# Exponentials three steps behind with sums by ScalarE, weights in fewer loads, and another order of the tail, in a top-k attention and feed-forward kernel

## The chip, the cores and the metric

One core of one Trainium2 chip. The metric is the time of one execution on the device in microseconds (us); less is better. Several runs of a kernel are given by their median with the lowest and the highest. The engines are named as the profile names them: PE is TensorE's matmul, PEld its weight load, DVE VectorE, ACT ScalarE, POOL GpSimd, SP SyncE (here only a queue for DMA).

## The reference

Eight batches of eight heads, 576 rows and 64 columns per head. Attention keeps only the 32 largest scores of each row; the result feeds a two-layer network with a squared relu.

```python
scores = scale * np.matmul(q, k.transpose(0, 1, 3, 2))
kth = np.partition(scores, -32, axis=-1)[..., -32:-31]
scores = np.where(scores >= kth, scores, -1000000000.0)
scores = scores - np.max(scores, axis=-1, keepdims=True)
attn = np.exp(scores)
attn = attn / (np.sum(attn, axis=-1, keepdims=True) + 1e-09)
out = np.matmul(attn, v)
x = out.transpose(0, 2, 1, 3).reshape(B * S, H * D)          # 4608 x 512
h = np.maximum(x @ w_in, 0.0)                                # 4608 x 2048
return h * h @ w_out                                         # 4608 x 512
```

## The kernel before

**Steps.** Heads go in pairs. The work is cut into U = 144 steps; a step holds two tiles of 128 query rows against all 576 keys of their heads (the list `steps`; a head's last 64 rows are joined with another's). One Python loop over `u` from 0 to 143 writes out the order of every engine by hand: each instruction goes through `pin`, which keeps it in program order on its engine. So an engine never overtakes: what stands behind a waiting instruction waits too. Tiles come from pools with a fixed number of buffers; a new tile waits for the last reader of the buffer that it takes.

**What happens to step w**, and in which turn of the loop:

- *Scores*, turn w - 1 (`scores`, L272). PE multiplies into two PSUM tiles `sc_a` and `sc_b` (L285), one for each half of the keys. ACT copies both into `s` (L294).
- *Candidates*, turn w - 1 and w (`pairs_of` L306, `quads_of` L319, `both` L332, `lesser` L340, `copy_far` L327). DVE takes maxima of pairs (L314, L315), then maxima and minima of quads (L323, L324) into `cat`. The minima of the pairs come from GpSimd (L338, L347), which needs a copy of one PSUM operand that ACT makes (`most`, L330). In the first EARLY = 11 steps DVE computes part of the minima itself (L317) and neither the copy nor the wider form on GpSimd is needed.
- *Top 32*, turn w (`topk`, L356). Four rounds of MAX8 on DVE (L374), with MATCH_REPLACE8 between them (L378), two tiles each. The largest and the 32nd value go to ACT, which negates them (`neg`, L394).
- *Dropping*, turn w + 1 (`drop`, L404). GpSimd writes for each score a number that is huge and negative where the score is below the 32nd (L409, tile `gone_a` or `gone_b`), and a DMA that accumulates adds it to `s` (L413). In the first EARLY - 2 steps GpSimd adds it itself (L411).
- *Exponentials*, turn w + 2 (`exps`, L415). ACT computes exp(s - max) into `w_two` (L417), one instruction for each of the two tiles; a DMA on SP transposes the result into `wT` (`turn`, L424).
- *Products*, turn w + 4 (`products` L796, `weigh` L452). PE multiplies `wT` with the values (L461) into the one PSUM tile `av_ps`. The values carry a 65th column of ones, so column 64 is the sum of the weights. DVE inverts it (`invert`, L473, reciprocal L475), and ACT scales by it into `x_tok` or `x_rem` (`place`, L483, L494).
- *Feed-forward*, spread over later turns (`x_unit`, `block`, `dense`). When a tile of 128 tokens is full it is transposed (L532) and copied (L538); then come 16 products of 128 x 128 per piece into a PSUM tile `gen` (L583), relu (L590) and square (L598) on ACT, and 16 accumulating products into `dn_ps` (L649), copied out and stored.

The order inside turn u is: drop(u - 1); quads and the first top-k round of u; scores(u + 1) with products(u - 4) between its two halves; invert and place of u - 4; exps(u - 2) and their transpose; DMA fetches of later heads (`fetch`); rounds two and three; the pair maxima of u + 1 and ACT's copy `most`; round four; ACT's `neg`; feed-forward pieces; one load of weights.

**Heads and weights.** `prepare` transposes the q and k of a pair of heads on PE and copies them on ACT, at turns given by `due`. The weights are cast while they are loaded, by DMAs that GpSimd issues (`load_weights`, L742): eight for `w_in`, of 64 rows each, and four for `w_out`. Three go out before the loop, then one per turn.

**The tail.** In the last two steps the masks are applied by DVE (`mask`, L419) to exponentials that ACT computes ahead (`early_exps`, L397), because the way over GpSimd and a DMA would be too long; PE transposes them (`turn_by_tensor`). From L873 on the remaining products, the last two tiles of tokens and their feed-forward pieces (`one`, `two`, `three`, `four`, then `fifth`, `sixth` and two more) are written out one by one. `one.bits(n)` gives the next n of the 16 products into `dn_ps` (L631); `homes` are PSUM homes for the first pieces.

Of the kernel before, what the change touches and what calls it, by code (L numbers as in the profile page):

```python
# [13 lines left out]
f32 = mybir.dt.float32  # L14
# [9 lines left out]
def kernel(  # L24
# [20 lines left out]
    def pin(ins):  # L45
        tc.keep_in_program_order(ins)
        return ins
# [80 lines left out]
    def fetch(n):  # L128
        while n and fetches:
            fetches.pop(0)[1]()  # L130
            n -= 1
# [140 lines left out]
    def scores(u, between=None):  # L272
        ps = [ps_sc.tile([128, 2, 512], f32, name=f"sc_{j}") for j in "ab"]
        js = (1, 0) if u < 2 else (0, 1)

        def half(j):
            for x, (i, c, a) in enumerate(steps[u]):
                qT, kT, bd, va = prep[i]
                k0 = j * HALF + 64 * (1 - x)
                if c < 4:  # L280
                    r = slice(64 * a, 64 * a + 64)
                    lhsT, rhs = qT[r, c * 128:(c + 1) * 128], kT[r, k0:k0 + HALF]
                else:
                    lhsT, rhs = bd[:, :], kT[:, k0:k0 + HALF]
                pin(nc.tensor.matmul(out=ps[j][:, x, 0:HALF], lhsT=lhsT, rhs=rhs, start=True, stop=True))  # L285

        half(js[0])
        if not between:
            half(js[1])
        s = scp.tile([128, 2, S], f32, name="s", bufs=4)  # L290
        st[u] = {"s": s, "ps": ps}
        st[u]["cat"] = scp.tile([128, 2, S], f32, name="cat", bufs=2)
        for j in js:
            pin(nc.scalar.activation(s[:, :, j * HALF:(j + 1) * HALF], ps[j][:, :, 0:HALF], AF.Copy))  # L294
            if u == 0 and j == 1:
# [51 lines left out]
        pin(tt(less, less, d["most"][:, 0:n_h, :, :].bitcast(i32).rearrange("p h x n -> p x h n"), op=ALU.subtract))  # L347

    GROUP = 18
    EARLY = 11  # L350
    held_m = {}
    tests = []

# [35 lines left out]
        return u == U - 1 or (u == U - 2 and x == 1)  # L389

    def negate(u, ends):
        neg = small.tile([128, 2, 2], f32, name="neg", bufs=4)
        got = st[u]["ends"] if ends == 2 else st[u]["ends"][:, :, 0:1]
        pin(nc.scalar.activation(neg[:, :, 0:ends], got, AF.Copy, scale=-1.0))  # L394
        return neg

    def early_exps(u, x):  # L397
        d = st[u]
        if "e" not in d:
            d["e"], d["neg_e"] = {}, negate(u, 1)  # L400
        e = d["e"][x] = scp.tile([128, S], bf16, name="e", bufs=3)
        pin(nc.scalar.activation(e[:, :], d["s"][:, x, :], AF.Exp, bias=d["neg_e"][:, x, 0:1]))
# [11 lines left out]

    def exps(u, x):  # L415
        d = st[u]
        pin(nc.scalar.activation(w_two[u % 3][:, x, 0:S], d["s"][:, x, :], AF.Exp, bias=d["neg"][:, x, 0:1]))  # L417

    def mask(u, x):  # L419
        d = st[u]  # L420
# [1 line left out]
                                           in1=d["e"][x][:, :], op0=ALU.is_ge, op1=ALU.mult))  # L422

    def turn(u):  # L424
        wT = scp.tile([128, 9, 128], bf16, name="wT", bufs=3)
        pin(nc.sync.dma_start_transpose(out=wT[:, :, :], in_=w_two[u % 3][:, :, :].rearrange("p x n -> p (x n)")))
        st[u]["wT"] = wT

# [5 lines left out]

    def turn_by_tensor(u, x):
        if "tp" not in st[u]:
            st[u]["wT"] = scp.tile([128, 9, 128], bf16, name="wT", bufs=3)
# [33 lines left out]
        return last_two[u][:, 0:130].rearrange("p (x d) -> p x d", x=2)  # L471

    def invert(u):  # L473
        r = small.tile([128, 2, 1], f32, name="rsum", bufs=4)
        pin(nc.vector.reciprocal(r[:, :, :], sums(u)[:, :, 64:65]))  # L475
        st[u]["r"] = r
# [3 lines left out]

    full = []

    def place(u, by_vec=False):  # L483
        for x, (i, c, a) in enumerate(steps[u]):
            b, pr = pairs[i]
            o, r = sums(u)[:, x, :], st[u]["r"]
            if c < 4:
                if (b, c) not in x_tok:
                    x_tok[b, c] = ffp.tile([128, 512], bf16, name="x_tok", bufs=8)
                h = 4 * (pr // 2) + 2 * a + pr % 2  # L490
                if by_vec:
# [206 lines left out]
    def most_ups(u):  # L698
        if u < U - 26:
            return 1 if downs else 2  # L700
        return 2 if u >= U - 20 or len(ups) > 4 else 1

    def in_gap(u):
        products(u - 4)
        if moves:
            moves.pop(0)()()

# [24 lines left out]

    w_loads = []
    for kh in range(KH):
        for e in range(2):
            rows = moe_w_in.rearrange("(t e a d) n -> t a e d n", t=2, e=2, a=2)[kh // 2, kh % 2, e]
            w_loads.append((w_in[64 * e:64 * e + 64, kh, :], rows))
    for g in range(4):
        rows = moe_w_out.rearrange("(f p) n -> p f n", p=128)[:, 4 * g:4 * g + 4, :]
        w_loads.append((w_out[:, 4 * g:4 * g + 4, :], rows))  # L740
# [14 lines left out]
    def due(i):  # L755
        if i >= NP - 8:
            return 101 + 4 * (i - (NP - 8))
        return first[4 * (i // 4) + 3] - 1 - 4 * (3 - i % 4) if i >= 4 else 3 * i + 2

    def prepare(u):  # L760
        nonlocal coming
# [11 lines left out]
    ones = const.tile([128, 1], f32, name="ones")  # L773
    pin(nc.gpsimd.memset(ones[:, :], 1.0))
    worst = const.tile([128, 1], f32, name="worst")
    load_weights(2)
    scores(0)
    both(0)
    copy_far(0)
# [8 lines left out]
    def ok(w):  # L788
        return 0 <= w < U
# [6 lines left out]
    def products(w):  # L796
        if ok(w):
            for x in range(2):
                weigh(w, x)

    def turn_x(u):
        for b, c in full:
            x_unit(u, b, c)
        full.clear()

    for u in range(U):
# [13 lines left out]
            both(u + 1)  # L820
        if u == 0:
            in_gap(u)
        if ok(u - 4):
            invert(u - 4)
# [3 lines left out]
        if ok(u - 4):  # L828
            place(u - 4)
        turn_x(u)  # L830
        moves.extend(soon_moves)
        soon_moves.clear()
        if ok(u - 2):
            exps(u - 2, 0)
            exps(u - 2, 1)
            turn(u - 2)
        fetch(4 if u < 12 else 3)
        topk(u, (1, 2))
        if u == U - 2:
            while behind:  # L840
# [12 lines left out]
        if u == U - 2:  # L853
            place(u - 3)
            turn_x(u)
            take("d", True)
            early_exps(u, 1)
            moves.pop(0)()()
        topk(u, (3,))
        if casts_next:  # L860
            prepare(u)
# [4 lines left out]
        if u < U - 2:  # L866
            dense(u, 0)
        st[u]["neg"] = negate(u, 2)
        if u < U - 2:
            dense(u, 1)  # L870
        load_weights(1)

    assert len(ups) == 4 and not downs and len(behind) == 1 and not fresh and not moves and not soon_moves  # L873
    by_hand.append(True)
    two_banks = ps_sc.tile([128, 2, 512], f32, name="sc_a")
    homes.extend(two_banks[:, z, :] for z in range(2))
    one, two = ups.pop(0)(), ups.pop(0)()
    behind.pop(0)()
    one.relu()
    three = ups.pop(0)()  # L880
    products(U - 4)
    four = ups.pop(0)()
    for x in range(2):
        exps(U - 3, x)
    turn(U - 3)
    exps(U - 2, 0)
    one.square(nc.gpsimd)
    two.relu()
    two.square(nc.gpsimd)
    early_exps(U - 1, 0)  # L890
    early_exps(U - 1, 1)
    topk(U - 1, (1, 2, 3))
    one.bits(4)
    three.relu()
    three.square(nc.gpsimd)
    while tests:
        pin(tests.pop(0)())
    mask(U - 2, 1)
    mask(U - 1, 0)
    mask(U - 1, 1)  # L900
# [7 lines left out]
    turned(U - 1, 0, False)  # L908
    products(U - 3)
    turn_by_tensor(U - 1, 1)  # L910
    turned(U - 1, 1, True)
    products(U - 2)
    invert(U - 4)
    invert(U - 3)
    invert(U - 2)
    place(U - 2, True)
    products(U - 1)
    invert(U - 1)
    place(U - 4)
    place(U - 3)  # L920
    place(U - 1, True)
    one.bits(2)
    by_hand.clear()
    late.append(True)
    turn_x(U)
    by_hand.append(True)
    move = moves.pop(0)()
    four.relu()
    late.clear()
    four.square()  # L930
    late.append(True)
    one.bits(2)
    move()
    tail.append(0)
# [4 lines left out]
    fifth.square()  # L939
    sixth = ups.pop(0)()  # L940
    sixth()
    one.bits(4)
    ups.pop(0)()()
    one.bits(4)
    ups.pop(0)()()
# [137 lines left out]
```

## Time and profile before

| | |
|---|---|
| median of 3 runs | 905.44 us (904.69 to 906.34) |
| the profiled execution's own time | 910.4 us |
| its span, first to last instruction | 908.3 us |
| mean granted clock of PE | 0.939 |
| accumulating DMA of `gone_b` into `s`, from issue to landing | 4.5 us median |

The page gives, for one profiled execution, the busy time of each engine, the span in 40 slices, the DMA queues, the chain of work that ended last, and the costliest groups of instructions with the idle time of the engine before them. A group's mean duration is the time from an instruction's start to its end; instructions of one engine overlap, so what an instruction takes of the engine's stream is read from the starts of its neighbours, in the chain or in the timeline. Times in the timeline are us from the start of the span.

### The profile page before, as it was taken

To read this page: it belongs to the slowest core of one execution; us is meant where nothing else is said; L and a number is where in the kernel's file an instruction comes from. 1 tells how busy PE (TensorE), PEld (TensorE's weight loads), DVE (VectorE), ACT (ScalarE), POOL (GpSimd) and SP (SyncE) were. 2 spreads that over 40 slices of the span, in tenths; PEclk is the share of its full clock that TensorE was granted. 3 is DMA by queue.
4 is the path that set the end of the run, shared out by engine and by line. 5 is a ranking of instruction groups with operands and counts; after the bars stand their busy time and mean duration, and the time that the engine had idled before them with its cause. 6 is when DMAs were issued, how large, how long until landed. Compare 5 with 4: busy or idle time off the path is not lost.

```text
span 908.3 us, 20985 instructions
## 1 busy us (share of the span) xinstructions
PE 683.6 (75%) x6264; PEld 426.1 (47%) x6264; DVE 878.8 (97%) x3629; ACT 761.2 (84%) x1755; POOL 780.7 (86%) x821
## 2 busy tenths in 40 slices
PE   6675867777777768777777677787777768887886
PEld 3332445444444445454454444554544444554554
DVE  6998999999999999999999999999999999999994
ACT  3564799889988898888998899888998888997894
POOL 7997889988898888888889888888898898899881
PEclk9999899999999998999998999989999899999998
DMA  7699898889988999899999988989799999787771
GB/s 146 105 165 147 189 187 196 191 193 209 196 189 172 193 206 195 186 184 200 198 190 196 197 195 195 193 194 202 183 202 199 198 205 211 151 169 164 166 162 40
DMA packets 290776, 164.78 MB, mean 181 GB/s; under 512 B 258144, under 2 KB 268640, under 8 KB 290656
## 3 DMA queue, kind: packets, MB, share of 16 engines
q1 hardware_dynamic: 267408, 80.29, 46.2%
q0 software_dynamic: 21904, 82.65, 40.7%
q8 instruction: 52, 0.85, 0.4%
q14 instruction: 68, 0.56, 0.2%
q10 hardware_dynamic: 1344, 0.43, 0.2%
HBM read 37.75 MB, written 9.44 MB: 52 GB/s over the span
## 4 chain that ended last, share of the span: by engine, by line
DVE 62%; issue 12%; ACT 7%; PE 4%; POOL 3%; DMA 2%; POOLq 0%; ACTq 0%
DVE m L374 25%; DVE cat L378 17%; DVE sc_b L314 6%; DVE most L315 4%; DVE cat L323 4%; DVE cat L324 4%; ACT s L294 1%; PE sc_b L285 1%; POOL cat L347 1%; DVE rsum L475 1%; ACT rl L590 1%; ACT x_tok L494 1%; DMA s<-gone_a 1%; ACT w_two_a L417 1%; PE gen L583 1%
## 5 line engine op out<-in xcount | busy, mean ns | idle before, releaser
L374 DVE MAX8 m<-cat 128x8 f32<-128x104 f32 (+3 forms) x1152 | 436.7, 419 | 0.0
L378 DVE MATCH_REPLACE8 cat<-m,cat 128x104 f32<-128x104 f32 (+2 forms) x864 | 261.5, 308 | 0.0
L338 POOL TENSOR_TENSOR cat<-s 128x576 int32<-128x576 int32 (+1 forms) x144 | 238.6, 1657 | 2.8 <-ACT s L294 2.8
L347 POOL TENSOR_TENSOR cat<-cat,most 128x576 int32<-128x576 int32 (+1 forms) x144 | 196.0, 1361 | 31.8 <-ACT most L330 10.7
L285 PE MATMUL sc_b<-qkT 64*128 64x288 f32 x512 | 109.9, 505 | 88.2 <-DVE cat L324 84.1
L285 PE MATMUL sc_a<-qkT 64*128 64x288 f32 x512 | 98.2, 457 | 89.4 <-DVE most L315 35.2
L583 PEld LDWEIGHTS <-w_in 128*128 128x128 bf16 x2304 | 144.8, 101 | 41.7 <-issue 19.0
L649 PE MATMUL dn_ps<-w_out,h 128*128 128x512 bf16 x544 | 155.9, 417 | 1.8 <-ACT wide L657 1.8
L583 PE MATMUL gen<-xT,w_in 128*128 128x128 bf16 x1984 | 135.6, 224 | 3.3 <-ACT xT L538 1.8
L409 POOL TENSOR_SCALAR gone_a<-s,neg 128x576 uint8<-128x576 f32 x143 | 107.1, 749 | 15.5 <-ACT neg L394 4.1
L409 POOL TENSOR_SCALAR gone_b<-s,neg 128x576 uint8<-128x576 f32 x142 | 106.3, 749 | 12.2 <-ACT neg L394 0.3
L294 ACT ACTIVATE s<-sc_b 128x576 f32<-128x576 f32 x144 | 93.4, 648 | 27.8 <-PE sc_b L285 24.0
L285 PEld LDWEIGHTS sc_a<-qkT 64*128 64x128 f32 x512 | 41.6, 188 | 116.8 <-issue 35.4
L294 ACT ACTIVATE s<-sc_a 128x576 f32<-128x576 f32 x144 | 91.3, 634 | 3.2 <-DVE cat L317 1.7
L285 PEld LDWEIGHTS sc_b<-qkT 64*128 64x128 f32 x512 | 45.0, 203 | 103.7 <-PE av_ps L461 62.5
L394 ACT ACTIVATE neg<-m 128x4 f32<-128x4 f32 (+1 forms) x145 | 29.9, 206 | 72.0 <-DVE m L374 70.6
L598 ACT ACTIVATE h<-rl 128x512 bf16<-128x512 f32 x137 | 86.3, 630 | 4.3
L590 ACT ACTIVATE rl<-gen 128x512 f32<-128x512 f32 x140 | 81.9, 585 | 1.8 <-PE gen L583 1.7
L461 PEld LDWEIGHTS <-wT 128*128 128x128 bf16 (+1 forms) x1600 | 55.3, 101 | 57.9 <-issue 45.8
L649 PEld LDWEIGHTS <-h 128*128 128x128 bf16 x544 | 52.5, 106 | 63.5 <-issue 29.9
L413 POOL DMA_DIRECT2D s<-gone_b x67 | 59.3, 885 | 22.0 <-DVE m L374 9.9
L413 POOL DMA_DIRECT2D s<-gone_a x66 | 58.3, 884 | 20.4 <-DVE m L374 10.8
(177 smaller groups left out, 1261.0 us busy)
## 6 DMA issues: line engine op xcount, KB each, us to landing
s<-gone_b POOLq DMA_DIRECT2D x67, 576.0 KB, 4.5
s<-gone_a POOLq DMA_DIRECT2D x66, 576.0 KB, 4.6
v_raw<-in_v_dram SPq DMA_DIRECT2D x64, 128.0 KB, 3.1
k_raw<-in_k_dram SPq DMA_DIRECT2D x63, 128.0 KB, 3.3
q_raw<-in_q_dram SPq DMA_DIRECT2D x63, 128.0 KB, 3.0
out_dram<-wide SPq DMA_DIRECT2D x31, 256.0 KB, 3.0
v_raw<-in_v_dram SPq DMA_DIRECT2D x64, 32.0 KB, 3.0
w_in<-in_moe_w_in_dram POOLq DMA_DIRECT2D x8, 256.0 KB, 4.5
```

The source lines that it names most:

```text
L285: pin(nc.tensor.matmul(out=ps[j][:, x, 0:HALF], lhsT=lhsT, rhs=rhs, start=True, stop=True))
L294: pin(nc.scalar.activation(s[:, :, j * HALF:(j + 1) * HALF], ps[j][:, :, 0:HALF], AF.Copy))
L338: pin(tt(less, s[:, :, 0:wide].bitcast(i32), s[:, :, HALF:HALF + wide].bitcast(i32), op=ALU.add))
L347: pin(tt(less, less, d["most"][:, 0:n_h, :, :].bitcast(i32).rearrange("p h x n -> p x h n"), op=ALU.subtract))
L374: pin(nc.vector.max(out=m[r][:, x, :], in_=part(r, x)))
L378: pin(nc.vector.match_replace(out=part(r, x), in_to_replace=m[r][:, x, :], in_values=part(r, x), imm_value=NEG))
L409: pin(nc.gpsimd.tensor_scalar(byte[:, x, :, 1], s[:, x, :], scalar1=d["neg"][:, x, 1:2], scalar2=-HUGE, op0=ALU.add, op1=ALU.mult))
L413: pin(nc.gpsimd.dma_start(out=s[:, :, :].rearrange("p x n -> p (x n)"), in_=byte[:, :, :, :].rearrange("p x n two -> p (x n two)").bitcast ...
L583: pin(nc.tensor.matmul(out=hp[:, n * n_rows:(n + 1) * n_rows], lhsT=w_in[:, kh, (f0 + n) * 128:(f0 + n + 1) * 128], rhs=xt(kh), start=(kh ...
L590: pin(nc.scalar.activation(kept["rl"][:, :], hp, AF.Relu))
L598: pin(nc.scalar.activation(h2, flat, AF.Square))
L649: pin(nc.tensor.matmul(out=op[:, :], lhsT=held["h2"][:, f, c * 128:(c + 1) * 128], rhs=w_out[:, f, :], start=(f == 0), stop=(f == NF - 1)))
```

## The change

- *Exponentials*: `to_raise(u)` gives u - 3 up to turn CATCH = 133 and u - 2 after it; products, invert and place follow one turn later as well (`to_weigh`: u - 5, later u - 4). At turn 133 a second pair of exps is issued, at turn 134 a second set of products. `s` gets five buffers, `wT` four, `neg` six.
- *Sums*: for steps below SUMMED = 120 each exps instruction also writes the sum of its row (`accum_out`) into a small tile that two steps share, and `invert` takes one reciprocal of four numbers per row for two steps. From step 120 on it is as before.
- *EARLY* is 9.
- *Weights*: `w_in` goes in four loads of 128 rows, two of them before the loop; eight loads in all.
- *Fetches* stand ahead of the exps in turns 0 to 5; pairs 2 and 3 are prepared earlier (`due`).
- *Tail*: the first two pieces get a PSUM tile each; a third piece is multiplied earlier; eight `dn_ps` products go out before the transposes of the last exponentials, and four fewer near the end; DVE and ACT share copies and scalings differently; the fourth square goes from ACT to GpSimd.

```diff
-        s = scp.tile([128, 2, S], f32, name="s", bufs=4)
+        s = scp.tile([128, 2, S], f32, name="s", bufs=5)
...
-    EARLY = 11
+    EARLY = 9
...
+    SUMMED = U - 24
...
     def exps(u, x):
         d = st[u]
-        pin(nc.scalar.activation(w_two[u % 3][:, x, 0:S], d["s"][:, x, :], AF.Exp, bias=d["neg"][:, x, 0:1]))
+        if u % 2 == 0 and x == 0 and u < SUMMED:
+            d["sums"] = small.tile([128, 2, 2], f32, name="sums", bufs=4)
+            st[u + 1]["sums"] = d["sums"]
+        total = d["sums"][:, u % 2, x:x + 1] if u < SUMMED else None
+        pin(nc.scalar.activation(w_two[u % 3][:, x, 0:S], d["s"][:, x, :], AF.Exp, bias=d["neg"][:, x, 0:1], accum_out=total))
...
     def invert(u):
+        if u < SUMMED:
+            if u % 2 == 0:
+                both_r = small.tile([128, 2, 2, 1], f32, name="rboth", bufs=4)
+                pin(nc.vector.reciprocal(both_r[:, :, :, 0], st[u]["sums"][:, :, :]))
+                st[u]["r"], st[u + 1]["r"] = both_r[:, 0], both_r[:, 1]
+            return
...
+    CATCH = U - 11
+
+    def to_raise(u):
+        return u - 3 if u <= CATCH else u - 2
+
+    def to_weigh(u):
+        return u - 5 if u <= CATCH + 1 else u - 4
+
     def in_gap(u):
-        products(u - 4)
+        products(to_weigh(u))
...
     for kh in range(KH):
-        for e in range(2):
-            rows = moe_w_in.rearrange("(t e a d) n -> t a e d n", t=2, e=2, a=2)[kh // 2, kh % 2, e]
-            w_loads.append((w_in[64 * e:64 * e + 64, kh, :], rows))
+        rows = moe_w_in.rearrange("(t e a d) n -> t a e d n", t=2, e=2, a=2)[kh // 2, kh % 2]
+        w_loads.append((w_in[:, kh, :], rows))
...
-        return first[4 * (i // 4) + 3] - 1 - 4 * (3 - i % 4) if i >= 4 else 3 * i + 2
+        return first[4 * (i // 4) + 3] - 1 - 4 * (3 - i % 4) if i >= 4 else 2 * i + 3
...
-    load_weights(2)
+    load_weights(1)
...
-        if ok(u - 2):
-            exps(u - 2, 0)
-            exps(u - 2, 1)
-            turn(u - 2)
-        fetch(4 if u < 12 else 3)
+        if u < 6:
+            fetch(4)
+        w = to_raise(u)
+        if ok(w):
+            exps(w, 0)
+            exps(w, 1)
+            turn(w)
+        if u >= 6:
+            fetch(4 if u < 12 else 3)
...
-            early_exps(u, 1)
             moves.pop(0)()()
+        if u == CATCH:
+            exps(u - 2, 0)
+            exps(u - 2, 1)
+            turn(u - 2)
...
+        if u == CATCH + 1:
+            products(u - 4)
+            invert(u - 4)
+            place(u - 4)
+            turn_x(u)
...
-    two_banks = ps_sc.tile([128, 2, 512], f32, name="sc_a")
-    homes.extend(two_banks[:, z, :] for z in range(2))
-    one, two = ups.pop(0)(), ups.pop(0)()
+    homes.extend(ps_sc.tile([128, 2, 512], f32, name=name)[:, 0, :] for name in ("sc_a", "sc_b"))
+    one, two, three = (ups.pop(0)() for _ in range(3))
     behind.pop(0)()
     one.relu()
-    three = ups.pop(0)()
...
-    exps(U - 2, 0)
     one.square(nc.gpsimd)
     two.relu()
     two.square(nc.gpsimd)
+    exps(U - 2, 0)
...
-    one.bits(4)
-    three.relu()
-    three.square(nc.gpsimd)
-    while tests:
-        pin(tests.pop(0)())
+    one.bits(8)
...
-    turned(U - 1, 1, True)
+    turned(U - 1, 1, False)
     products(U - 2)
+    products(U - 1)
+    three.relu()
     invert(U - 4)
     invert(U - 3)
-    invert(U - 2)
-    place(U - 2, True)
-    products(U - 1)
-    invert(U - 1)
     place(U - 4)
     place(U - 3)
-    place(U - 1, True)
-    one.bits(2)
+    three.square(nc.gpsimd)
+    while tests:
+        pin(tests.pop(0)())
+    invert(U - 2)
+    place(U - 2, (True, True))
+    invert(U - 1)
+    place(U - 1, (True, False))
+    four.relu()
+    four.square(nc.gpsimd)
...
     sixth()
-    one.bits(4)
     ups.pop(0)()()
     one.bits(4)
```

More of the change, by code (lines that the diff above doesn't have):

```diff
@@ L391, in negate @@
     def negate(u, ends):
-        neg = small.tile([128, 2, 2], f32, name="neg", bufs=4)
+        neg = small.tile([128, 2, 2], f32, name="neg", bufs=6)
         got = st[u]["ends"] if ends == 2 else st[u]["ends"][:, :, 0:1]
@@ L424, in turn @@
     def turn(u):
-        wT = scp.tile([128, 9, 128], bf16, name="wT", bufs=3)
+        wT = scp.tile([128, 9, 128], bf16, name="wT", bufs=4)
         pin(nc.sync.dma_start_transpose(out=wT[:, :, :], in_=w_two[u % 3][:, :, :].rearrange("p x n -> p (x n)")))
@@ L436, in turn_by_tensor @@
         if "tp" not in st[u]:
-            st[u]["wT"] = scp.tile([128, 9, 128], bf16, name="wT", bufs=3)
+            st[u]["wT"] = scp.tile([128, 9, 128], bf16, name="wT", bufs=4)
             st[u]["tp"] = {}
@@ L481, with place @@
     full = []
-    def place(u, by_vec=False):
+    def place(u, by_vec=(False, False)):
         for x, (i, c, a) in enumerate(steps[u]):
@@ L490, in place @@
                 h = 4 * (pr // 2) + 2 * a + pr % 2
-                if by_vec:
+                if by_vec[x]:
                     pin(nc.vector.tensor_scalar(x_tok[b, c][:, h * 64:(h + 1) * 64], o[:, 0:64], scalar1=r[:, x, :], scalar2=None, op0=ALU.mult))
@@ L822 @@
             in_gap(u)
-        if ok(u - 4):
-            invert(u - 4)
+        if ok(to_weigh(u)):
+            invert(to_weigh(u))
         casts_next = bool(soon) and soon[0].__name__ == "values"
@@ L827 @@
             prepare(u)
-        if ok(u - 4):
-            place(u - 4)
+        if ok(to_weigh(u)):
+            place(to_weigh(u))
         turn_x(u)
@@ L868 @@
         st[u]["neg"] = negate(u, 2)
+        if u == CATCH + 1:
[3 more added lines that the diff above has]
+            turn_x(u)
         if u < U - 2:
             dense(u, 1)
+        else:
+            early_exps(u, 1)
         load_weights(1)
@@ L926 @@
     by_hand.append(True)
+    one.bits(2)
     move = moves.pop(0)()
[L928 to L931, printed above, removed]
     one.bits(2)
```

## The prediction

> **What bounds the kernel now.** I read the page from the top (busy shares, chain, groups), then the windows, then single steps in the chain and the timeline.
>
> ```profile
> span 908.3 us, 20985 instructions
> PE 683.6 (75%) x6264; PEld 426.1 (47%) x6264; DVE 878.8 (97%) x3629; ACT 761.2 (84%) x1755; POOL 780.7 (86%) x821
> DVE 62%; issue 12%; ACT 7%; PE 4%; POOL 3%; DMA 2%; POOLq 0%; ACTq 0%
> ```
> ```profile
> 300.00:400.00 100.00, 75.17 (x696) 47.92 (x694) 99.25 (x409) 87.89 (x202) 87.80 (x88) 0.91 0.89 191
> ```
>
> VectorE (DVE) is 97% busy and 99.25 of 100 us in the middle: it is the bound. ScalarE (ACT, fourth pair of numbers) has 12.1 us per 100 left. A step, from one `L323` to the next, is 6.00 us; one step in the chain:
>
> ```profile
> 302.67 0.36 DVE cat L323
> 303.03 0.36 DVE cat L324
> 303.39 0.33 DVE m L374 x2
> 303.73 0.47 DVE cat L378 x2
> 304.20 0.08 DVE rsum L475
> 304.28 0.36 DVE m L374 x2
> ...
> 308.67 0.35 DVE cat L323
> ```
>
> The reader is to see the difference between a duration and a place in the stream: DVE instructions overlap, and the reciprocal, whose group row gives 156 ns, pushes the next maximum back by 0.08 us only.
>
> **The parts, each against this execution (910.4 us, of which 908.3 are the span).**
>
> *Reciprocals.* 120 steps had one each; now 60 cover two steps each. 60 go: 60 x 0.08 = **-4.8**. Twice the elements (four for two) I cost at nothing. By the 156 ns it would be 9.4; I take the place in the chain and keep 9.4 as an end.
>
> *EARLY from 11 to 9.* The two steps 9 and 10 lose their `L317` on DVE:
>
> ```profile
> 59.82 0.44 DVE L317 TENSOR_TENSOR cat<-sc_a,s 128x288 f32<-128x288 f32 x1
> 60.19 1.40 DVE L374 MAX8 m<-cat 128x8 f32<-128x576 f32 x2
> ```
>
> 0.37 apart, so **-0.7**. ACT gets two `L330`, GpSimd two wider pairs and, for steps 7 and 8, two DMA issues in place of four additions: work that other steps already carry beside a DVE of 6.00 us, cost 0; without that cover 0.4 each.
>
> *Exponentials one step later.* What this removes are waits of ACT for the accumulating DMA:
>
> ```profile
> 78.71 0.95 POOL L413 DMA_DIRECT2D s<-gone_b  x1 [0.31 <-DVE sc_b L314]
> 90.10 1.44 ACT L417 ACTIVATE w_two_a<-s,neg 128x576 bf16<-128x576 f32 x2 [6.52 <-DMA s<-gone_b]
> 91.87 0.46 DVE L323 TENSOR_TENSOR cat<-sc_b,most 128x288 f32<-128x288 f32 x1 [5.55 <-ACT most L330]
> 278.53 0.46 DVE L323 TENSOR_TENSOR cat<-sc_b,most 128x288 f32<-128x288 f32 x1 [0.54 <-ACT most L330]
> ```
> ```profile
> DVE rsum L475 <- PE av_ps L461: 1.1, 2, 0.7
> ```
>
> One DMA took 11.4 us (78.71 to 90.10); ACT had stood ready for its exps since 83.58, 5 us after the issue; in ACT's queue `L330` stood behind them, and DVE waited 5.55. With a step more there are 11 us, so what is left is under 0.4. The second such wait (0.54) goes too. The two waits of the reciprocal for TensorE (1.1 in all) go for another reason: the sum now comes from ACT, steps earlier. What is late next is the transposed tile `wT`; exps to products stays two steps, so that is no worse. Sum **-7.2**, bounds 0 (the DMA is not slow in other executions) and -7.2.
>
> *The cost: 240 exps write a sum.* The built program has one ACT instruction more behind each of them, which reads the accumulator, for steps 0 to 119. The trace has none. The nearest row is the smallest ACT instruction:
>
> ```profile
> 308.71 0.21 ACT L394 ACTIVATE neg<-m 128x4 f32<-128x4 f32 x1 [0.69 <-DVE m L374]
> 308.82 0.58 ACT L590 ACTIVATE rl<-gen 128x512 f32<-128x512 f32 x1
> 305.42 1.45 ACT L417 ACTIVATE w_two_a<-s,neg 128x576 bf16<-128x576 f32 x2
> ```
> ```profile
> L417 ACT ACTIVATE w_two_a<-s,neg 128x576 bf16<-128x576 f32 x96 | 69.6, 786 | 7.2 <-DMA s<-gone_b 7.2
> L394 ACT ACTIVATE neg<-m 128x4 f32<-128x4 f32 (+1 forms) x145 | 29.9, 206 | 72.0 <-DVE m L374 70.6
> ```
>
> It holds the stream for 0.11 us and lasts 0.21. Lower end 0 (hidden in the exp's own end), upper end 0.30 (its whole 0.21, and most of the 0.12 by which two exps of 0.786 overlap in 1.45). I take 0.10 as nearest, 0.20 per step. It is free only where ACT is early. The place that decides is `L330`, which stands right behind the exps and which DVE's `L323` waits for:
>
> ```profile
> 307.08 0.41 ACT L330 ACTIVATE most<-sc_b 128x288 f32<-128x288 f32 x1 [0.21 <-DVE sc_b L314]
> 308.59 0.44 DVE L323 TENSOR_TENSOR cat<-sc_b,most 128x288 f32<-128x288 f32 x1
> ...
> 314.17 0.41 ACT L330 ACTIVATE most<-sc_b 128x288 f32<-128x288 f32 x1
> 314.62 0.46 DVE L323 TENSOR_TENSOR cat<-sc_b,most 128x288 f32<-128x288 f32 x1
> ```
>
> Here 1.10 us of room in one step, 0.04 in the next. Over the 110 steps from 10 to 119 (first and last pair: 78.69 and 80.24, 740.98 and 742.20) the room averages 0.68; it is under 0.2 in 15 steps, under 0.4 in 23, under 0.5 in 33. What is missing sums to 2.2 us for 0.2 more per step, 6.0 for 0.4, 8.8 for 0.5. Lateness that ACT's idle time in a step does not absorb goes into the next; carrying it gives 2.7, 9.7 and 14.8. So **+2.7**, bounds 0 and 21 (0.3 per read).
>
> *Catch-up at step 133, spare buffers, fetches ahead of exps, preparation earlier.* The extra exps (1.45) and products stand on ACT around one `neg`, where ACT waits for DVE 70.6 us in all (row above), and early ACT is busy for 15.98 of 25 us:
>
> ```profile
> 25.00:50.00 25.00, 16.97 (x106) 8.57 (x105) 25.00 (x101) 15.98 (x38) 23.45 (x27) 1.00 0.66 122
> ```
>
> Cost 0; if that cover is gone, 1.5. A transpose on SP now stands behind four fetches in steps 0 to 5, with two steps until its products.
>
> *Weights in four loads.* POOL saves four issues of 0.57; it is not the bound, 0. The bytes are the same. The rival below is about the engines that carry them.
>
> *Tail.* Near the end the chain is TensorE without a gap:
>
> ```profile
> 895.45 0.86 PE dn_ps L631 x4
> 896.31 0.89 PE end L583 x16
> 897.20 0.86 PE dn_ps L631 x4
> 898.07 0.89 PE gen L583 x16
> ```
>
> One of the two `dn_ps` groups moves ahead of the last transposes: -0.86. Before that, ACT waited for both halves of one PSUM tile:
>
> ```profile
> 883.43 0.60 ACT L590 ACTIVATE rl<-sc_a 128x512 f32<-128x512 f32 x1 [1.45 <-PE sc_a L583]
> 887.44 1.54 DVE L421 SCALAR_TENSOR_TENSOR w_two_c<-s,m,e 128x576 bf16<-128x576 f32 x2 [0.74 <-ACT e L402]
> ```
>
> With two tiles the relu starts 16 products (0.89) sooner, and with it the exps and `e` behind it on ACT; DVE has 0.74 of idle for `e` to give, and the chain from the masks to the xT copy moves up by about 0.9. The new wait: eight `dn_ps` products in a row wait for GpSimd's second square, with the transposes of `w_two_b` queued behind on TensorE; that square comes sooner too, as its relu moves ahead of one exp, and I take it that the products end when the masked tile is ready. **-1.8**; bounds 0 (the eight products hold the transposes up by the 0.9) and -2.3.
>
> **Sum.** -4.8 - 0.7 - 7.2 - 1.8 + 2.7 = -11.8: 910.4 becomes 898.6. Against the median of the runs shown, 905.44, the profiled execution is 5.0 longer. If those 5.0 are part of the 7.2 of waits, 2.2 are left to gain in a run without a profile: 905.44 - 4.8 - 0.7 - 2.2 - 1.8 + 2.7 = 898.6. Both ways lead to the same; I say **898.6**.
>
> **The rivals.**
>
> *The waits are in every run* and the 5.0 is the profiler's own: 905.44 - 11.8 = 893.6. For it: the three runs agree within 1.7 us, as they would with a regular stall. Against: one DMA that lasts 11.4 where the median is 4.5 looks like chance.
>
> *ACT becomes the bound (slower).* At `L423`, if a read costs 0.25, 0.5 per step: 14.8 in place of 2.7 gives 910.7; at 0.2, 9.7, 905.6. It decides from about 0.21 on, where the cost eats the other gains. For it: an `L394` lasts 0.21, and the accumulator can be read only after the exp has ended. Against: short ACT instructions overlap, 0.11 apart.
>
> *The large w_in loads run on few DMA engines.* Their source is two blocks of 64 rows, their destination 128 partitions. If such a load is dealt out by its two blocks, two engines carry 64 rows each:
>
> ```profile
> q0 software_dynamic: 152, 0.52, 54.7%
> ```
> ```profile
> q0 software_dynamic: 48, 0.18, 90.5%
> q1 hardware_dynamic: 7, 0.00, 1.1%
> ```
>
> From 8 to 14 us a packet of queue 0 took 0.547 x 16 x 6 / 152 = 0.35 us, so a load would hold its engines for 22 us instead of 3, until about 46 us for the last; and from 11.2 to 12.2 us, with that queue full, the q, k and v loads of queue 1 got 1.1%. The third pair's loads are wanted by its transposes,
>
> ```profile
> 37.70 0.66 PE L174 MATMUL gen<-id_f,q_raw 128*128 128x128 f32 x4
> ```
>
> and these move from step 4 to step 3, to about 31 us, a step earlier. An engine held from 8 to 30 us then still has most of that pair's packets to carry: about 3 us late, and as much for the fourth pair while the last load runs. Not all of it passes on to DVE: +4, bounds 0 and 8, so 902.6. The Trainium skill, "DMA: Bandwidth & Descriptors", section "Why a DMA increments its semaphore by 16 and not by 1", states such a rule: the largest number up to 16 that divides the slowest dimension of both sides, 2 here; it also names software-issued copies that get 16 all the same. The same page's "Rules for kernel authors" would have one transfer over 128 partitions and gives no gain for halves; by that alone the sum stays. No load of before has such a shape, so no row here decides.
>
> **How the numbers follow.** Forecast 0.48; waits in every run 0.14; costly reads 0.17 (slower 0.09, same 0.06, still faster 0.02); few engines 0.15 (faster 0.11, same 0.04); the rest, a tail or a phase that does not gain, 0.06 (faster 0.04, same 0.02). Faster by over 0.2% (about what a measurement of this kernel can tell from no change): 0.79, same 0.12, slower 0.09. The range reaches from the second case with cheap reads, 891, to reads of 0.2, 906.
>
> **What would show it.** DVE steps of 5.92 and 6.00 us in turn until step 119 and 6.00 after; no `L323` waiting over 1 us; an ACT group of 240 accumulator reads, 0.1 apart from what follows; exps without a DMA as releaser; the final run from the xT copy to the end shorter by 0.86. I am wrong if steps grow beyond 6.1 us until step 122 and shrink after it (reads), if packets of w_in still run after 40 us (engines), or if the transposes of `w_two_b` wait for a square (tail).

## The result and the profile after

The changed kernel takes 914.81 us (median of 6 runs, 913.76 to 918.18); the kernel before, on the same chip, 905.29 (904.33 to 907.53). The ratio is 1.0106 (95% interval 1.0086 to 1.0126): slower by 9.5 us, where 6.8 less than the median was forecast. The profiled execution of the changed kernel took 914.7 us, so it stands near its median; that of before stood 5 above.

First the head of the changed kernel's page, with its chain:

```profile
span 912.6 us, 20980 instructions
PE 671.4 (74%) x6190; PEld 424.8 (47%) x6268; DVE 873.8 (96%) x3567; ACT 779.4 (85%) x1996; POOL 778.2 (85%) x816
DVE 66%; issue 12%; ACT 10%; PE 5%; SPq 5%; DMA 2%; ACTq 0%
```

DVE does 5 us less work than before (878.8), as the removed instructions would have it, and yet the span is longer. New in the chain is SyncE's queue (SPq) with 5%, but that part of the chain hangs on a releaser that the landing times below do not bear out, so nothing is built on it here. To place the loss, take `L323` at the start of steps 8, 120 and 142 from the two timelines, before first:

```profile
61.52 0.43 DVE L323 TENSOR_TENSOR cat<-sc_b,most 128x288 f32<-128x288 f32 x1
...
742.20 0.43 DVE L323 TENSOR_TENSOR cat<-sc_b,most 128x288 f32<-128x288 f32 x1
...
874.53 0.45 DVE L323 TENSOR_TENSOR cat<-sc_b,most 128x288 f32<-128x288 f32 x1
```
```profile
77.39 0.44 DVE L323 TENSOR_TENSOR cat<-sc_b,most 128x288 f32<-128x288 f32 x1
...
747.85 0.43 DVE L323 TENSOR_TENSOR cat<-sc_b,most 128x288 f32<-128x288 f32 x1
...
881.30 0.43 DVE L323 TENSOR_TENSOR cat<-sc_b,most 128x288 f32<-128x288 f32 x1
```

Up to step 8: +15.9. Steps 8 to 120: 670.5 in place of 680.7, -10.2. Steps 120 to 142: +1.1. From there to the end of the span: 31.3 in place of 33.8, -2.5. The sum is +4.3, the difference of the spans. So the middle and the tail gained, and all that was lost was lost in the first 77 us. Of the 10.2 some 7 belong to that one execution of before: in e3_before_large, which has the steps of before from 8 to 120, the stretch lasts 673.8. The waits of the changed kernel from 30 to 62 us, each row with its total, count and longest:

```profile
ACT qkT L175 <- PE gen L174: 17.5, 2, 14.1
PE gen L174 <- DMA q_raw<-in_q_dram: 17.0, 2, 13.5
DVE sc_b L314 <- ACT s L294: 15.8, 1, 15.8
POOL gone_b L411 <- ACT neg L394: 15.1, 1, 15.1
PEld gen L174 <- DMA k_raw<-in_k_dram: 13.8, 1, 13.8
PEld gen L174 <- DMA q_raw<-in_q_dram: 3.9, 1, 3.9
```

It is one stall of 15.8 us in step 4: DVE waits for ACT, ACT for TensorE's transposes, and these for the third pair's q (3.5 us) and then for its k (13.5 us):

```profile
35.45 0.63 PE L174 MATMUL gen<-id_f,q_raw 128*128 128x128 f32 x4 [3.47 <-DMA q_raw<-in_q_dram]
49.61 1.11 PE L174 MATMUL gen<-id_f,k_raw 128*128 128x128 f32 x4 [13.54 <-DMA q_raw<-in_q_dram]
```

The PE rows put the second wait down to a q load, the PEld rows to a k load. PEld is right: these transposes read `k_raw`, and the pair's second large k load, issued at 27.41, landed 22.2 us later, at 49.57. Why q and k are late stands in SyncE's timeline, of the changed kernel first, then of before. The columns are start, the time that the issuing instructions took, and how many they are:

```profile
12.03 1.82 SPq L110 DMA_DIRECT2D q_raw<-in_q_dram  x2
13.89 10.85 SPq L117 DMA_DIRECT2D q_raw<-in_q_dram  x1
24.79 6.74 SPq L110 DMA_DIRECT2D k_raw<-in_k_dram  x2
31.57 1.98 SPq L117 DMA_DIRECT2D k_raw<-in_k_dram  x1
33.66 1.23 SPq L108 DMA_DIRECT2D v_raw<-in_v_dram  x2
34.93 6.05 SPq L117 DMA_DIRECT2D v_raw<-in_v_dram  x2
41.08 6.03 SPq L110 DMA_DIRECT2D q_raw<-in_q_dram  x2
49.59 1.23 SPq L117 DMA_DIRECT2D q_raw<-in_q_dram  x1
```
```profile
12.06 1.24 SPq L110 DMA_DIRECT2D q_raw<-in_q_dram  x2
13.35 0.67 SPq L117 DMA_DIRECT2D q_raw<-in_q_dram  x1
14.05 0.60 SPq L110 DMA_DIRECT2D k_raw<-in_k_dram  x1
...
29.81 0.59 SPq L110 DMA_DIRECT2D k_raw<-in_k_dram  x1
30.45 0.64 SPq L117 DMA_DIRECT2D k_raw<-in_k_dram  x1
```

The third pair's q goes out at 12.03 and its k at 24.79 to 31.57; what goes out at 41.08 is the fourth pair's q. The DMA view gives the time from issue to landing of these loads, two rows of the changed kernel first (issues from 8 to 14 and from 26 to 32 us), then the same of before:

```profile
q_raw<-in_q_dram SPq DMA_DIRECT2D x2, 128.0 KB, 22.7
k_raw<-in_k_dram SPq DMA_DIRECT2D x2, 128.0 KB, 20.3
```
```profile
q_raw<-in_q_dram SPq DMA_DIRECT2D x2, 128.0 KB, 5.9
k_raw<-in_k_dram SPq DMA_DIRECT2D x1, 128.0 KB, 4.5
```

So q was issued as early as before and landed 17 us later: the transfer is slow. The issue is slow too: one 32 KB load takes 10.85 us to issue in place of 0.67, and SyncE issues in order. This pushes k's first load from 14.05 to 24.79, but its last ones, at 29.81 and 30.45 in before, by little. How much of k's lateness comes from the late issue and how much from the slow transfer is not separated in this kernel; g1_one_two_block and h1_alone below say more. What fills the DMA engines meanwhile is in the DMA view, changed kernel from 8 to 48 us, and 8 to 14 us in the last two rows (columns: issues and KB each, then median us from issue to landing; for a queue packets, MB and share of 16 engines):

```profile
w_in<-in_moe_w_in_dram POOLq DMA_DIRECT2D x4, 512.0 KB, 24.6
```
```profile
q1 hardware_dynamic: 2685, 0.82, 58.1%
q0 software_dynamic: 923, 0.06, 15.1%
```

A load of twice the bytes takes 24.6 us where 4.5 was the median in the same stretch of before. And queue 0 carries 923 packets with 0.06 MB, where before it carried 152 with 0.52: most of them are packets of 4 bytes. From 8 to 62 us the trace holds 3680 such packets, for 6 weight loads; the run by halves below has 128 for 8 loads, 16 each. 3680 - 6 x 16 = 3584 = 4 x 14 x 64: each two-block load gives 14 engines 64 packets without data, and leaves 64 rows to each of the other two. The trace does not name the engine of a packet, so this is read from counts. A second count agrees: of the 4 KB packets of queue 0, 2.0 are in flight on average from 12 to 14 us, some 6 from 20 to 24, when three loads are under way, 7.9 from 26 to 32, with four, and 2.0 again from 40 to 46, with the last one: two per load.

### The profile page after: what moved, and what is told of

Same layout as the page of the kernel before. It is cut to its first block, busy times and chain, and to the rows that moved or that the text cites. A ratio compares the mean times of both kernels' runs of the same rounds, so it can differ in the third digit from the quotient of the medians.

```text
span 912.6 us, 20980 instructions
## 1 busy us (share of the span) xinstructions
PE 671.4 (74%) x6190; PEld 424.8 (47%) x6268; DVE 873.8 (96%) x3567; ACT 779.4 (85%) x1996; POOL 778.2 (85%) x816
## 4 chain that ended last, share of the span: by engine, by line
DVE 66%; issue 12%; ACT 10%; PE 5%; SPq 5%; DMA 2%; ACTq 0%
DVE m L374 28%; DVE cat L378 18%; DVE sc_b L314 6%; DVE most L315 5%; DVE cat L324 5%; DVE cat L323 5%; SPq L117 2%; ACT s L294 2%; SPq L110 1%; ACT h L610 1%; DMA q_raw<-in_q_dram 1%; ACT rl L602 1%; PE dn_ps L661 1%; PE sc_b L285 1%; PE gen L595 1%
## 5 line engine op out<-in xcount | busy, mean ns | idle before, releaser
L285 PE MATMUL sc_b<-qkT 64*128 64x288 f32 x512 | 105.8, 488 | 87.6 <-DVE cat L324 83.6
L595 PEld LDWEIGHTS <-w_in 128*128 128x128 bf16 x2304 | 149.0, 102 | 41.5 <-issue 20.3
L661 PE MATMUL dn_ps<-w_out,h 128*128 128x512 bf16 x478 | 143.0, 421 | 10.6 <-issue 6.8
L595 PE MATMUL gen<-xT,w_in 128*128 128x128 bf16 x1984 | 137.6, 226 | 3.5 <-ACT xT L550 2.9
L411 POOL TENSOR_SCALAR gone_b<-s,neg 128x576 uint8<-128x576 f32 x142 | 105.9, 746 | 29.1 <-ACT neg L394 17.5
L294 ACT ACTIVATE s<-sc_b 128x576 f32<-128x576 f32 x144 | 93.2, 647 | 22.2 <-PE sc_b L285 16.3
L314 DVE TENSOR_TENSOR sc_b<-sc_a,s 128x288 f32<-128x288 f32 x144 | 65.3, 454 | 18.8 <-ACT s L294 16.3
L661 PEld LDWEIGHTS <-h 128*128 128x128 bf16 x544 | 51.8, 105 | 64.0 <-issue 31.3
## 6 DMA issues: line engine op xcount, KB each, us to landing
w_in<-in_moe_w_in_dram POOLq DMA_DIRECT2D x4, 512.0 KB, 24.6
```

Source lines behind the costliest of these rows:

```text
L314: pin(tt(far, one[:, :, QUAR:HALF], two[:, :, QUAR:HALF], op=ALU.max))
L411: pin(nc.gpsimd.tensor_scalar(byte[:, x, :, 1], s[:, x, :], scalar1=d["neg"][:, x, 1:2], scalar2=-HUGE, op0=ALU.add, op1=ALU.mult))
L595: pin(nc.tensor.matmul(out=hp[:, n * n_rows:(n + 1) * n_rows], lhsT=w_in[:, kh, (f0 + n) * 128:(f0 + n + 1) * 128], rhs=xt(kh), start=(kh ...
L661: pin(nc.tensor.matmul(out=op[:, :], lhsT=held["h2"][:, f, c * 128:(c + 1) * 128], rhs=w_out[:, f, :], start=(f == 0), stop=(f == NF - 1)))
```

## The experiments

Letters in the expectations: A, a two-block load is carried by two DMA engines and blocks the loads behind it; B, the accumulator reads ate the gain; C, large loads as such; D, the earlier preparation. F and G came later. All edits are to the changed kernel if nothing else is said; "before" is its run on the same chip. The groups of runs were measured on different chips, on which the kernel before took 905.18 (e1 to e4), 904.92 (f1 to f4), 904.22 (f5, f6, g1, g2) and 903.83 us (h1, h2), so a difference of about 1 us between runs of different groups shows nothing.

**Eight loads again (e1_eight).** The loop of before in place of the new one, and `load_weights(2)` ahead of `scores(0)`.

> The changed kernel (914.8 us) with w_in in eight loads of 64 rows again. Theory A (a two-block load is carried by two DMA engines and blocks the q, k and v loads): step 4 goes back from 22.2 us to about 6.3, w_in lands in about 4.5 us, and the time is 914.8 - 15.8 = 899.0 (897 to 901). Theory B (the accumulator reads cost what was lost): no more than 2 us are gained, 913. Theory D (the earlier preparation of the third pair is what stalls): step 4 still stalls by several us, 905 to 915.

Measured: 904.03 us (897.45 to 907.96 without the profiled execution, which took 919.5); ratio 0.9963 (0.9928 to 0.9999). Step 4 took 6.30 us and w_in landed in 4.6, as A has it. But the time is 5 above A's and scatters over 10 us. The profiled execution, the longest of all eleven, lost 22 us in steps 10 to 13, in the chain at

```profile
66.12 11.46 DMA wT<-w_two_c
77.58 11.96 DMA wT<-w_two_a
...
94.97 19.66 DMA wT<-w_two_c
```

A second thing is wrong in this kernel; it is taken up by f4_eight_early11. That the shorter executions lose their time at the same place is not shown.

**Four large loads of another shape (e2_by_halves).**

```diff
-    for kh in range(KH):
-        rows = moe_w_in.rearrange("(t e a d) n -> t a e d n", t=2, e=2, a=2)[kh // 2, kh % 2]
-        w_loads.append((w_in[:, kh, :], rows))
+    for t in range(2):
+        for e in range(2):
+            rows = moe_w_in.rearrange("(t e a d) n -> t e d a n", t=2, e=2, a=2)[t, e]
+            w_loads.append((w_in[64 * e:64 * e + 64, 2 * t:2 * t + 2, :], rows))
```

> The changed kernel with four loads of 512 KB still, but each into 64 partitions with two rows of 4 KB per partition, so that the slowest dimension is 64 and not 2. Theory A: no stall in step 4, landing 7 to 10 us (twice the bytes of the 4.5 us loads), 899 (897 to 902). Theory C (large loads as such fill the engines): the landing stays above 20 us and so does the stall, 910 to 915.

Measured: 897.31 us (896.34 to 899.18); before 905.18; ratio 0.9903 (0.9876 to 0.9930). The DMA view from 8 to 48 us and the windows of 30 to 50 us, this run first, then the changed kernel (DVE is the third pair of numbers):

```profile
w_in<-in_moe_w_in_dram POOLq DMA_DIRECT2D x4, 512.0 KB, 6.8
```
```profile
30.00:40.00 10.00, 7.51 (x38) 3.99 (x38) 10.00 (x46) 6.49 (x17) 9.40 (x11) 1.00 0.73 113
40.00:50.00 10.00, 6.32 (x51) 3.42 (x51) 10.00 (x36) 7.00 (x19) 9.31 (x12) 1.00 1.15 174
```
```profile
30.00:40.00 10.00, 1.86 (x8) 1.10 (x8) 10.00 (x45) 2.00 (x4) 7.53 (x9) 0.81 0.89 154
40.00:50.00 10.00, 0.39 (x2) 0.39 (x3) 0.14 (x1) 0.00 (x0) 0.00 (x0) 0.50 0.64 115
```

The same number of loads, the same bytes, packets of 4 KB in both: what differs is which dimension stands outermost, and with it the number of partitions that a load fills (64 in place of 128), and 17.5 us come back. The partitions are not it: the loads of w_out, 512 KB into 128 partitions too, land after 6.6 us in the kernel before. C falls, A stands. This kernel computes all that the reference asks and is faster than both.

**The large loads in the kernel before (e3_before_large).** The two-block loop and one load ahead of `scores(0)`.

> The kernel before (905.3 us) with the four two-block loads alone. Theory A: SyncE's issues block as in the changed kernel, q of the third pair lands at about 49 us where its transposes want it at 37.7, so the time grows by 9 to 16, to 914 to 921. Theory D: the preparation is not earlier here, so no stall: 905. Theory B: 905.

Measured: 924.52 us (923.31 to 926.10), ratio 1.0202 (1.0142 to 1.0262): +19.3, more than A's 16. Step 4 took 25.0 us and step 5 8.2 in place of 6.3 each. What TensorE waited for here was not q, as A has it, but a transposed tile `wT`, for 19.8 us: its issue stood 13.2 us in SyncE's queue, and it landed 26.5 us after the issue began. B and D fall: the loads alone cost it all.

**Preparation where it was (e4_due).** `due` back at `3 * i + 2`, large loads kept.

> The changed kernel with the large loads kept and the preparation of pairs 1 to 3 put back to where it was (one step later for the third pair). Theory A: the landing of q sets the end of the stall, whichever step asks for it, so at most 3 us come back: 911 to 915. Theory D: 899.

Measured: 915.68 us (914.98 to 916.93). The stall only moves to step 5 (24.2 us in place of 6.4). D falls.

**The price of the sums (f1_no_sums, f2_sums_unused),** on the loads by halves.

```diff
-    SUMMED = U - 24
+    SUMMED = 0                      (f1)
-        if u < SUMMED:
+        if u < 0:                   (f2, in invert alone)
```

> The changed kernel with the w_in loads by halves (897.3 us), but without the sums: no exp writes a sum, and each step takes its own reciprocal from PSUM again (120 in place of 60). By the forecast's terms 60 reciprocals at 0.08 come back (+4.8) and 240 reads at 0.10 go (-2.7): 899.4. If the reads are free: 902.1. If a read costs 0.25 (-14.8): 887.

> As the run without sums, but the 240 exps still write their sums, which nobody reads; 120 reciprocals from PSUM. Against the loads by halves (897.3) only the reciprocals differ: +4.8 by their place in the stream, 902.1; +9.4 by their duration, 906.7. Against the run without sums only the accumulator reads differ: +2.7 by the forecast, 0 if they are free, +14.8 if ScalarE is the bound.

Measured: 901.49 (900.14 to 902.47) without sums, 903.11 (900.61 to 906.47) with sums that nobody reads, ratios 0.9957 (0.9941 to 0.9973) and 0.9980 (0.9961 to 0.9998). So 240 reads cost 1.6 (from step 8 to 120, by `L323`: 674.2 and 676.0), and 60 reciprocals 5.8 against the loads by halves (676.0 and 670.5). The intervals of the two ratios overlap a little, and one trace tells little: in the ten other traces of kernels with sums and with exponentials three steps behind (e1_eight with its jam left out) this stretch lasts from 669.1 to 672.0. So the reciprocals' gain is clear, and the price of the reads is small, but not clear of noise. A pair of exps with their reads in ACT's timeline of the changed kernel:

```profile
309.09 0.78 ACT L423 ACTIVATE w_two_b<-s,neg 128x576 bf16<-128x576 f32 x1
309.76 0.21 ACT L423 ACTIVATION_READ_ACCUMULATOR w_two_b<-s,neg 128x1 f32 x1
309.85 0.78 ACT L423 ACTIVATE w_two_b<-s,neg 128x576 bf16<-128x576 f32 x1
310.52 0.20 ACT L423 ACTIVATION_READ_ACCUMULATOR w_two_b<-s,neg 128x1 f32 x1
310.61 0.41 ACT L330 ACTIVATE most<-sc_b 128x288 f32<-128x288 f32 x1
```

A read lasts 0.21 us, but what follows starts 0.09 after it: its place in the stream is 0.09.

**Exps two steps behind (f3_two_behind),** on the loads by halves: `CATCH = -99`.

> The loads by halves (897.3) with the exponentials two steps behind all the way, as in the kernel before, and so no catch-up at step 133. By the forecast's second way (most of the waits for the accumulating DMA occur in the profiled run of before alone) 0 to 2.2 come back: 897.3 to 899.5. If the waits are in every run (the rival): 904.5.

Measured: 900.21 us (898.55 to 901.45), ratio 0.9949 (0.9932 to 0.9966): by the medians the third step is worth 2.9, its catch-up included. Its waits show what it removes, here the largest two of five such groups; in the run by halves one wait of 1.7 is left:

```profile
ACT w_two_b L423 <- DMA s<-gone_a: 4.6, 4, 1.6
ACT w_two_a L423 <- DMA s<-gone_a: 3.6, 5, 1.3
```

Many waits of about 1 us, and none of 5. How they reach DVE the trace does not show: its `L323` waits 1.8 us for `L330` here and 1.6 in the run by halves.

**Eight loads, EARLY 11 (f4_eight_early11).** e1_eight with `EARLY = 11`.

> The changed kernel with eight loads of w_in (median 904.0, runs from 897.4 to 908.0) and EARLY at 11 again, so that the accumulating DMAs begin in step 9 and not in step 7, when the last w_out load is gone. Theory F (the jam of steps 10 to 13 in that run is w_out loads, which eight w_in loads push to step 8, beside the accumulating DMAs that EARLY 9 brings forward): narrow runs near 897.3 + 0.7 = 898.0 (897 to 899.5). If eight loads are at fault by themselves: again 903 to 905, with the same spread.

Measured: 897.81 us (897.21 to 899.15). The scatter is gone. In e1_eight the last two w_out loads went out at 63.05 and 69.63 and the first accumulating DMAs at 65.80 and 72.36; here the DMAs begin at 78.61. So with EARLY 9 the loads must be few: four of them bring the last w_out load forward to 50.63.

**EARLY by itself (f5_halves_early11, g2_halves_early7),** on the loads by halves.

> The loads by halves (897.3 us) with EARLY back at 11. By the forecast two DVE minima of 0.37 come back: 898.0. If EARLY 9 also costs somewhere (two more copies on ScalarE, two more accumulating DMAs): 897 or less.

> The loads by halves (897.3 us) with EARLY at 7, so that the first accumulating DMA goes out at about 52 us, while the last w_out load (50.6 to 57) is under way. Two more minima saved: 896.6 if nothing jams. By theory F (w_out loads beside accumulating DMAs jam): over 899 with a spread of several us, as the eight loads with EARLY 9 had, though with one load beside them in place of two.

Measured: 898.08 (896.34 to 902.19) with 11, 897.31 with 9, 897.46 (896.05 to 898.58) with 7. From 11 to 9 the medians differ by 0.8, within the spread and across two chips; in the traces the two steps are shorter by 0.37 and 0.36, as forecast. From 9 to 7 nothing is gained. F in its simple form falls: with 7 an accumulating DMA went out at 52.87 beside a w_out load from 50.12, and nothing jammed. In e1_eight two of each went out within 10 us; how many it takes stays open.

**The tail's four products (f6_bits),** on the loads by halves: `one.bits(8)` becomes `one.bits(4)`, and `one.bits(4)` stands behind `sixth()` again.

> The loads by halves (897.3 us) with the four dn_ps products of the tail moved back to where they stood before (behind the sixth group instead of ahead of the transposes). By the forecast +0.86: 898.2. If the eight products hold the transposes up by as much: 897.3.

Measured: 898.50 us (896.32 to 901.39). From `L323` of step 142 to the end of the span 31.7 us in place of 31.3: 0.4 by the trace, where the medians say 1.2 and the spread and the change of chip cover both.

**One two-block load (g1_one_two_block).** The first quarter of w_in as in the changed kernel, the second in two loads of 64 rows, the other half by halves.

> The changed kernel with one two-block load (the first) and the other three quarters of w_in in loads of 64 partitions. Theory A (each two-block load holds two engines for some 22 us, and SyncE's issues stand behind them): packets of the one load end at about 33 us instead of 47 for four, q of the third pair lands some 14 us sooner, so step 4 stalls by 0 to 2 us: 897.3 to 899.5. If one such load blocks as long as four: 912.

Measured: 910.65 us (909.19 to 912.48). A miss: one load costs 13.3, four 17.5. TensorE waits 12.7 us for the third pair's q here and only 0.9 for its k. The two large q loads went out at 12.02 and 12.62, as in before, and landed some 30 us later, so SyncE's slow issue, which came behind them, has no part in this wait. The DMA view from 20 to 26 us (the busy share of the 16 engines in tenths, and GB/s):

```profile
DMA  2011110203011130111111112011111199990251
GB/s 61 0 41 27 34 27 7 61 0 68 0 34 27 29 89 2 34 27 29 34 29 34 29 61 56 0 29 27 29 29 29 27 166 84 84 166 0 58 82 29
```

In most slices two engines of 16 (one tenth) move 29 GB/s and little else moves. 512 KB at 29 GB/s is 18 us, but the jam lasts longer: the same rate holds again from 36 to 40 us, after the two-block load has landed at 34.7, as if two engines still had shares of other loads to carry. Two runs asked why.

**That load alone, and that load last (h1_alone, h2_last).** h1 holds all other weights back until step 4 (`if u >= 4: load_weights(1)`, no second load ahead of the loop, `EARLY = 13`); h2 sends the same five loads with the two-block one last.

> One two-block load of w_in as in the run with one, but all other weights are held back until step 4 and later (and EARLY is 13, so that w_out does not meet the accumulating DMAs: about 1.5 us more in steps 9 to 12). Theory G (the shares of the other weight loads stand behind it on its two engines): the pair is free at about 8.5 + 18 = 27 us plus the shares of q, k and v, SyncE's blocked issues end before 32 us, and the stall in step 4 falls from 12.5 to 4 or less. If one load blocks by itself: the stall stays at 10 to 13.

> The same five loads of w_in, the two-block load last, at about 30 us, when the third pair's q, k and v have been issued (they were issued by 28 us in the run with loads by halves). Theory G: no stall in step 4; its pair of engines is held from 30 to about 48 us, so the next pair's loads, w_out and the transposed tiles meet it there, with a stall of 0 to 8 us in steps 5 to 7. If the place makes no difference: 12 us in steps 5 to 7.

Measured: h1 901.34 us (899.36 to 905.43), of which some 1.5 belong to EARLY 13; step 4 takes 7.4 us, a stall of 1.1 in place of 12.5. Of the 4.0 us against the loads by halves, measured on another chip, the rest stays open. The load itself still lands after 24.7 us, and the issue behind it still takes 10.86, as in g1_one_two_block, but TensorE's wait for q falls from 12.7 to 1.6. So G holds: one load jams so long because the shares of the loads behind it queue on its two engines. h2: 914.12 us (913.32 to 914.92, two runs). Step 4 is free, as expected, but steps 5 and 6 stall by 14.7 and 1.8: TensorE waited 16.2 us for a transposed tile `wT`, which landed 23.1 us after its issue. More than the 8 expected; the place changes who waits, and does not make it cheaper.

## Why the prediction was wrong, point by point

- *Weights in four loads*: the step that failed. "POOL saves four issues of 0.57; it is not the bound, 0. The bytes are the same." The number of issues and bytes was counted, not how a load is dealt out to the engines; measured, a loss of 15.8 in the trace (step 4) and of 17.5 against as many loads by halves. The cause in its place: each load lies on two engines for some 24 us, and the loads of q and k behind it land 20 to 23 us after their issue in place of 4 to 6.
- *The rival "few DMA engines"* had the right mechanism and the wrong size and chance: +4 with bounds 0 to 8, at 0.15. It reckoned the load's hold of its engines well (22 us; 24.6 to landing) and its sign came, with packets of w_in until 47 us. It put the third pair about 3 us late, and q was: TensorE waited 3.5 us for it. What it left out is k, 13.5 us more: k's large loads were issued at 24.79 and 27.41, behind the fourth two-block load (23.59, landed at 47.7), and landed at 43.3 and 49.6. Part of this is SyncE's slow issue (10.85 us); in the run by halves the same loads go out at 15.28 and 15.87. But the slow issue is not needed for a stall: g1_one_two_block has one of 12.5 us from q loads issued on time.
- The rule that this rival named, in the Trainium skill, "DMA: Bandwidth & Descriptors", section "Why a DMA increments its semaphore by 16 and not by 1", is borne out by the counts: 2 divides the two blocks and the 128 partitions, and two packets with data are in flight per load. The Trainium skill asks on the same page, under "Rules for kernel authors", in another row for a dimension that is a multiple of 16 outermost; e2_by_halves does that, and its loads land in 6.8 us in place of 24.6. The Trainium skill's row there on one 128-partition transfer, which was set against the rule, says nothing of the outermost dimension and decided nothing here.
- *Reciprocals* -4.8: measured 5.8 (5.5 in the trace). Right, by the place in the stream: steps take 5.93 and 6.00 us in turn, as was said; by their duration it would have been 9.4.
- *Reads* +2.7, 0.10 each: 1.6 by the medians, not clear of noise, and 0.09 each in the stream; a read's row starts 0.11 before that of its exp ends. The rival of costly reads (14.8) falls.
- *Waits* -7.2 in the profile, of which 2.2 in other runs: 2.9. The size is about right, the picture only in part: one long wait of one execution was chance, as the second way of the sum had it (steps 8 to 120 last 680.7 there and 673.8 in e3_before_large), but the waits that stay are many and short, and the forecast had not seen them.
- *EARLY* -0.7: 0.73 in the steps themselves, 0.8 by the medians, within the spread. What it cost at nothing, the two accumulating DMAs more, is free only with the w_out loads out of the way.
- *Tail* -1.8: the tail after step 142 is shorter by 2.5, of which the four `dn_ps` products seem to carry 0.4 to 1.2 where 0.86 was put; from the xT copy to the end it is 14.5 in place of 15.3. The transposes did not wait for the square.
- *Steps 120 to 142* +1.1, where 0 was put for the catch-up. f3_two_behind, without it, has 132.1 there like before (132.3), but runs with the catch-up have from 131.8 (e4_due) to 133.5, so what it costs, within its bound of 1.5, is not shown.
- The sum without the failed step, 898.6, against 897.31 for the kernel that has all the rest and loads of another shape. That these agree so well is in part luck: measured one by one the five parts add up to a gain of 10.4, and together they gave 7.9 on e2_by_halves' chip, where 6.8 was forecast.

## What to carry to other kernels

Before merging DMAs, look at the outermost dimension of both sides, not at bytes and issues: if it is 2, as here, two engines carry the load, and everything that is dealt to all engines afterwards ends with these two. Ask of each late wait when its load was issued and when it landed, and do not take the releaser that one row names for granted: here a row named q where k was meant. Ask for each queue, too, what stands behind an issue that takes 11 us. Two edits of one change can need each other (four loads and EARLY 9), so undo them together as well as one by one.

## What the runs showed of the hardware

- An issuing instruction on SyncE, mostly 0.5 to 1.3 us, took 10.85 to 10.86 in five kernels (changed, e3_before_large, e4_due, g1_one_two_block, h1_alone), each time the same 32 KB load, the eighth that SyncE issued behind the first two-block load; a transpose's issue took 13.2 (e3_before_large), and that of another 32 KB load 10.68 (h2_last). That the engines' queues were full is argued from this, not shown.
- Two engines alone move 29 GB/s with 4 KB packets (h1_alone, 20 to 26 us; g1_one_two_block, 36 to 40 us). With four two-block loads under way 7.9 such packets were in flight on average (changed kernel, 26 to 32 us), so they did not share one pair.
- An accumulator read on ACT lasts 0.21 us and takes 0.09 of the stream.
